# Partly accumulating transfers for the in-place additions of the last two layers, the last product cut in two, and a new order

## The chip, the cores and the metric

The kernel runs on one core of a Trainium2 chip. The metric is the time of one execution in device microseconds (us), the median of several runs. The core has a matrix engine (TensorE; PE in the profile, its weight loads PEld), VectorE (DVE), ScalarE (ACT) and GpSimd (POOL). SyncE (SP) issues the transfers between memory and the core. In the kernel before, GpSimd issues none.

## The reference

Three layers run one after the other on 2 batches of 768 tokens.

```
1. attention, 8 heads of 64: a window of +-15 keys, plus the maxima of 24 blocks of 32 keys; softmax; times v and block means
2. four causal attention experts of width 64 (q, k, v, output matrix); the two experts with the largest gate logits are summed
3. x_prev = x shifted by one token;  xk = mu_k*x + (1-mu_k)*x_prev,  xr likewise with mu_r
   k = max(xk @ w_k, 0);   v = (k*k) @ w_v;   out = sigmoid(xr @ w_r) * v
```

The third layer has 512 model columns and 1024 hidden ones. `w_k`, `w_v` and `w_r` come as 64-bit floats.

## The kernel before

All products keep nearly full precision: each operand is split into a rounded part and a rest (`halves`: a rounding, then a subtraction), and a product is three matmuls. The two large products of the third layer, `hid` (x times `w_k`) and `duo` (k*k times `w_v`), are built from seven products of half size in place of eight, with extra additions of operands and of partial results. A partial result comes out of one of eight PSUM banks by `copy` (ScalarE), `plus` or `plus_in` (VectorE, which alone adds from PSUM in these steps). Additions of two partial results that both lie in SBUF are `more(x, y)`, x += y: 8 for each of the two calls of `hid` (128 x 384 each) and 2 for each of the six calls of `duo` (128 x 256 each). `result` multiplies a finished quarter with the gate and stores it.

Every step is an operation with one or several ways to do it, an engine for each. `op` notes them in program order with what they read and write. `Plan.run` then issues them in the order of the list ORDER. An entry of ORDER divided by four is the number of the operation, and the remainder is its way. HOMES gives each buffer a place. Each engine runs its own instructions strictly in that order, and waits where an operand or a place isn't ready. The costs that the operations carry served the search for ORDER; they have no effect on the chip.

`more` was built with `both`, which has two ways, an addition on VectorE or the same on GpSimd. The last call of `duo` ends with a product of 256 columns (12 matmuls), `plus`, `result` and its store.

Of the kernel before, what the change touches and what calls it, by code (L numbers as in the profile page):

```python
# [20 lines left out]
P = 128  # L21
# [15 lines left out]
C = 384  # L37
# [277 lines left out]
def attn_moe_rwkv(  # L315
# [739 lines left out]
    def both(eng, dst, a, b, n, fn, r, w):  # L1055

        any_of(eng, [("dve", dve(n), lambda: nc.vector.tensor_tensor(dst(), a(), b(), fn), True),  # L1057
                     ("pool", pool_tt(n), lambda: nc.gpsimd.tensor_tensor(dst(), a(), b(), fn))], r=r, w=w)

    def flat64(w, k):  # L1060
        return raw64(w[k * P:(k + 1) * P].rearrange("p (m c) -> p m c", m=1))

# [423 lines left out]
```

## Time and profile before

| | |
|---|---|
| time, median of 3 runs | 333.79 us (331.25 to 334.03) |
| the profiled execution's own time | 333.63 us |
| its span, first to last instruction | 331.8 us |
| granted TensorE clock | 1.0 of full in the whole span |
| busy: TensorE, VectorE, ScalarE, GpSimd | 95%, 93%, 81%, 32% |

The span is the time from the first to the last instruction; the execution's own time has 1.8 us around it. Busy shares count overlapping instructions of an engine once. A busy TensorE may still hold short waits, since matmuls are pipelined, so its chain and its waits are read beside it.

### The profile page before, as it was taken

The numbers are of one execution on the slowest core, as the hardware profiler recorded it, in microseconds if no ns is written. First come the engines' busy times: TensorE is split into PE (matmuls) and PEld (weight loads), VectorE is DVE, ScalarE is ACT, GpSimd is POOL, SyncE is SP. The second block draws the span as 40 slices with busy tenths as digits, with TensorE's granted clock in tenths as the row PEclk, the third lists the DMA queues.
The fourth block names the chain that finished last, engine by engine and source line by source line (L and its number), as shares of the span: only waits on it lengthen the run. The fifth ranks groups of instructions, "written<-read, shape, count | busy, mean of one in ns | idle before, by whom it ended". The sixth has DMA issues, their size and how long they took to land.

```text
span 331.8 us, 8988 instructions
## 1 busy us (share of the span) xinstructions
PE 314.3 (95%) x3296; PEld 284.9 (86%) x3296; DVE 309.4 (93%) x936; ACT 267.6 (81%) x779; POOL 107.6 (32%) x128
## 2 busy tenths in 40 slices
PE   0769999999999999999999999999999999999995
PEld 0659998888799879888777899999997899999994
DVE  1988999999999899999999999999999999999995
ACT  1687989999999979597988897696997788967540
POOL 0563783784342632332400012142431302030121
PEclk9999999999999999999999999999999999999999
DMA  7996898854331101011212201000122000011123
GB/s 257 360 405 208 271 359 288 284 138 137 119 122 31 37 1 38 29 64 65 67 62 65 64 0 61 4 0 3 63 63 66 0 0 5 30 65 35 63 81 111
DMA packets 19735, 34.19 MB, mean 103 GB/s; under 512 B 2116, under 2 KB 8516, under 8 KB 19692
## 3 DMA queue, kind: packets, MB, share of 16 engines
q1 hardware_dynamic: 19692, 33.62, 30.6%
q8 instruction: 26, 0.43, 0.5%
q14 instruction: 17, 0.14, 0.1%
HBM read 30.13 MB, written 3.15 MB: 100 GB/s over the span
## 4 chain that ended last, share of the span: by engine, by line
PE 78%; DVE 16%; issue 2%; DMA 2%; ACT 1%; SPq 0%; DVEq 0%
PE ps L1282 18%; PE ps L752 11%; PE ps L1144 10%; PE ps L635 6%; PE ps L950 6%; PE ps L770 6%; PE ps L852 6%; PE ps L992 5%; PE ps L677 4%; PE ps L1195 4%; PE ps L581 3%; DVE b L376 2%; DVE t L1121 2%; DVE b L1057 2%; DMA ks<-in_kS 2%
## 5 line engine op out<-in xcount | busy, mean ns | idle before, releaser
L1282 PE MATMUL ps<-w,s 128*128 128x256 f32 x336 | 48.6, 281 | 0.0
L1282 PEld LDWEIGHTS ps<-w,s 128*128 128x128 f32 x336 | 43.9, 188 | 0.1
L1195 PE MATMUL ps<-b,w 128*128 128x384 f32 x216 | 40.6, 337 | 0.0
L368 ACT ACTIVATE t<-ps 128x192 f32<-128x192 f32 (+1 forms) x109 | 31.1, 347 | 9.6 <-PE ps L635 5.3
L1195 PEld LDWEIGHTS ps<-b,w 128*128 128x128 f32 x216 | 38.1, 188 | 0.1
L752 PE MATMUL ps<-b,w 128*128 128x384 f32 x192 | 37.3, 341 | 0.0
L1144 PE MATMUL ps<-w,b 128*128 128x512 f32 x144 | 35.5, 397 | 0.6 <-DVE b L1168 0.6
L752 PEld LDWEIGHTS ps<-b,w 128*128 128x128 f32 x192 | 33.1, 188 | 0.6 <-issue 0.2
L1144 PEld LDWEIGHTS ps<-w,b 128*128 128x128 f32 x144 | 26.5, 188 | 6.9 <-DVE b L1168 1.0
L368 ACT ACTIVATE b<-ps 128x384 f32<-128x384 f32 (+4 forms) x55 | 26.0, 489 | 6.7 <-PE ps L1195 2.7
L607 ACT ACTIVATE w<-w,nm 128x120 f32<-128x120 f32 x72 | 27.9, 391 | 0.0
L378 POOL TENSOR_TENSOR b<-t,b 128x384 fp32r<-128x384 f32 x7 | 9.2, 1315 | 49.5 <-DVE b L369 33.3
L368 ACT ACTIVATE b<-t 128x384 fp32r<-128x384 f32 x40 | 20.1, 522 | 4.9 <-DVE t L1121 2.5
L852 PE MATMUL ps<-ks,b 64*128 64x384 f32 (+3 forms) x192 | 21.0, 341 | 0.0
L368 ACT ACTIVATE s<-u 128x512 fp32r<-128x512 f32 x24 | 14.7, 625 | 7.8 <-DVE u L1057 5.3
L1121 DVE SCALAR_TENSOR_TENSOR t<-b,mu,t 128x384 f32<-128x384 f32 x32 | 20.9, 669 | 0.0
L368 ACT ACTIVATE w<-ps 120x256 f32<-120x256 f32 (+2 forms) x50 | 19.5, 430 | 1.6 <-PE ps L635 0.9
L950 PE MATMUL ps<-t,b 128*64 128x384 f32 (+2 forms) x144 | 20.8, 422 | 0.0
L376 DVE TENSOR_TENSOR b<-t,b 128x384 fp32r<-128x384 f32 x37 | 20.4, 563 | 0.0
L770 PE MATMUL ps<-q,b 128*128 128x260 f32 x144 | 19.7, 287 | 0.0
L992 PE MATMUL ps<-u,w 128*128 128x384 f32 x96 | 19.6, 339 | 0.0
L770 PEld LDWEIGHTS ps<-q,b 128*128 128x128 f32 x144 | 18.3, 188 | 0.6 <-issue 0.3
(200 smaller groups left out, 896.8 us busy)
## 6 DMA issues: line engine op xcount, KB each, us to landing
s<-in_wk SPq DMA_DIRECT2D x8, 512.0 KB, 4.0
s<-in_wv SPq DMA_DIRECT2D x8, 512.0 KB, 3.8
w<-in_vp SPq DMA_DIRECT2D x15, 256.0 KB, 6.1
w<-in_qT SPq DMA_DIRECT2D x12, 256.0 KB, 5.3
out_y<-t SPq DMA_DIRECT2D x24, 128.0 KB, 1.7
s<-in_wr SPq DMA_DIRECT2D x4, 512.0 KB, 5.5
s<-in_kS SPq DMA_DIRECT2D x6, 320.0 KB, 6.0
ks<-in_kS SPq DMA_DIRECT2D x4, 400.0 KB, 6.1
```

Of the source, the lines that this page charges most:

```text
L368: ways = [("act", act(n, sb), lambda: nc.scalar.activation(dst(), src(), AF.Copy)), ("dve", dve2(n) if sb else dve(n), lambda: nc.vector.t ...
L376: ways = [("dve", dve(n), lambda: nc.vector.tensor_tensor(dst(), a(), b().bitcast(F32), ALU.subtract), sb)]
L607: op("act", act(NK, True) + 186, lambda i=i, z=z, pr=pr, nm=nm: nc.scalar.activation(pr()[:, i], pr()[:, i], AF.Exp, bias=nm.t[:, i:i + 1] ...
L752: mm(p.t[:, :C], a[kc].t[:, cols], x.t[:, kc, :], start=(kc == 0 and i == 0), stop=(kc == KC - 1 and i == 2))
L770: mm(p.t[:, :260], x.t[:, kc, tok], a[kc].t, start=(kc == 0 and i == 0), stop=(kc == KC - 1 and i == 2))
L852: mm(ps[e2].t[:, :z - a], q1.t[r, x, tok], ks.t[r, y, a:z], start=n == 0, stop=n == 2)
L950: mm(acc.t[64 * e2:64 * e2 + 64, tq0 * P:(tq0 + cnt) * P], vv.t[:, kb, e * D:(e + 1) * D], th[e2].t[:, i0 * P:(i0 + cnt) * P], start=first ...
L992: mm(p.t[:, :C], a[ep].t[:, m * P:(m + 1) * P], x.t[:, ep, :], start=(ep == 0 and i == 0), stop=(ep == 1 and i == 2))
L1121: op("dve", dve(C) + 60, lambda: nc.vector.scalar_tensor_tensor(tmp(), cur(), mu.t[:, i:i + 1], tmp(), ALU.mult, ALU.add), r=rd, w=[(mb, m ...
L1144: mm(p.t, a.t[:, kc, tok], w[2](), start=(kc == 0 and i == 0), stop=(kc == KC - 1 and i == 2))
L1195: mm(p.t[:, :C], a[2]()[:, o:o + P], x.t[:, u, j], start=not (j or i), stop=j == 1 and i == 2)
L1282: mm(p.t[:, :256], x.t[:, u, j * P:(j + 1) * P], v[2]()[:, col:col + 256], start=not (j or i), stop=j == FC // 2 - 1 and i == 2)
```

## The change

1. `more` is built with a new `onto`, which has a third way: a transfer issued by GpSimd that adds y onto x on its way into x. It is noted with 900 ns on GpSimd and 4500 ns more until x can be used.
2. The last product of the last `duo` is cut into two of 128 columns, each with its own `plus`, `result` and store.
3. The cost of the score matmuls of layer 2 for the search is lowered and their kind is named "scores" in place of "rows".
4. ORDER and HOMES are new.

```
+    def onto(x, y, n):
+
+        any_of("dve", [
+            ("dve", dve(n), lambda: nc.vector.tensor_tensor(x[2](), x[2](), y[2](), ALU.add), True),
+            ("pool", pool_tt(n), lambda: nc.gpsimd.tensor_tensor(x[2](), x[2](), y[2](), ALU.add)),
+            ("pool", 900, lambda: nc.gpsimd.dma_start(x[2](), y[2](), accum_op=ALU.add), False, 4500.0),
+        ], r=[y[:2]], w=[x[:2]])
...
-                    op("pe", max(3 * pe_r(z - a) + 107.0, 385.0), go,
+                    op("pe", max(3 * pe_r(z - a), 330.0), go,
...
         def more(x, y):
-            both("dve", x[2], x[2], y[2], C, ALU.add, [y[:2]], [x[:2]])
+            onto(x, y, C)
...
         def more(x, y):
-            both("dve", x[2], x[2], y[2], 256, ALU.add, [y[:2]], [x[:2]])
+            onto(x, y, 256)
...
-        plus(u2, product(operand(s), 1, 256), 256)
-        result(ta, 256, u2)
+        n = P if tb == B * TPB - 1 else 256
+        x = operand(s)
+        for col in range(0, 256, n):
+            y = (u2[0], col, lambda col=col: u2[2]()[:, col:col + n]) if n < 256 else u2
+            plus(y, product(x, 1, 256 + col, n), n)
+            result(ta, 256 + col, y, n)
```

Of the 28 additions, 20 have remainder 2 in the new ORDER, so they become transfers: 14 of the 16 in `hid` (entries 5866, 5906, 5870, 5886, 5846, 5910, 5890, 5850 in the first call, 6414, 6434, 6378, 6398, 6418, 6438 in the second) and 6 of the 12 in `duo` (7322, 7326, 7658, 7662, 7826, 7830). Before, 16 of these 20 were on VectorE and 4 on GpSimd. These lines of the new list hold three of them (5890, 5850, 6414) and 5968, the `plus` that reads what 5890 has added to:

```
+    6032, 6132, 6904, 5780, 5890, 6236, 6921, 6016, 6104, 7056, 5850, 6177, 6140, 5784, 6220, 7060, 5952, 6152,
+    6340, 6144, 6020, 6160, 6004, 7064, 6024, 6241, 7068, 5964, 6036, 6448, 7148, 6445, 5976, 6228, 5968, 6630,
...
+    6710, 7009, 7124, 6742, 7025, 6364, 5948, 6408, 7028, 6384, 6744, 6414, 6200, 7156, 6192, 6368, 6480, 7100,
```

In the whole kernel, the two lists name these numbers of instructions: TensorE 2740 before and 2752 after (matmuls and transposes), VectorE 776 and 765 operations, ScalarE 581 and 571, GpSimd 124 and 144 (20 of them the transfers), SyncE 118 and 122 transfers.

## Rows read from the trace of the kernel before

**Rows 1.** The page: busy time of each engine, and two engines in 40 slices.
```profile
PE 314.3 (95%) x3296; PEld 284.9 (86%) x3296; DVE 309.4 (93%) x936; ACT 267.6 (81%) x779; POOL 107.6 (32%) x128
...
PE   0769999999999999999999999999999999999995
...
DVE  1988999999999899999999999999999999999995
```

**Rows 2.** The chain that ended last: start us, us, what, in order of time.
```profile
1.64 5.60 DMA ks<-in_kS
7.27 2.55 DVE ksm L487 x3
...
15.56 1.63 issue
...
21.95 2.23 issue
...
107.63 1.05 PE ps L992 x6
...
124.76 1.25 PE ps L992 x6
...
214.65 1.40 DVE ks L1168 x3
...
253.91 12.06 PE ps L1144 x51
...
270.89 56.99 PE ps L1282 x480
```

**Rows 3.** Windows of two stretches of `hid`: busy us of each engine, clock, DMA.
```profile
220.00:230.00 10.00, 10.00 (x59) 10.00 (x58) 10.00 (x19) 8.67 (x19) 3.97 (x4) 1.00 0.01 2
230.00:240.00 10.00, 9.65 (x55) 9.32 (x54) 10.00 (x21) 8.53 (x19) 3.78 (x3) 1.00 0.16 52
```

**Rows 4.** Waits of TensorE's matmuls from 24 us on, all of them: total, times, longest.
```profile
PE ps L581 <- issue: 2.2, 1, 2.2
PE ps L1144 <- DVE b L1168: 0.6, 1, 0.6
PE ps L1195 <- DVE b L1213: 0.4, 1, 0.4
```

**Rows 5.** Additions, by line and shape, 200 to 271 us: busy us, mean ns.
```profile
L1057 DVE TENSOR_TENSOR b<-b,b 128x384 f32<-128x384 f32 x9 | 5.6, 641 | 0.0
...
L1058 POOL TENSOR_TENSOR b<-b,b 128x384 f32<-128x384 f32 x3 | 4.4, 1467 | 14.7 <-DVE b L1057 8.9 <-DVE ks L1213 5.8
...
L1168 DVE TENSOR_TENSOR b<-ps,b 128x384 f32<-128x384 f32 x15 | 7.5, 542 | 0.0
```

**Rows 6.** GpSimd's additions of 128 x 256 by line, 230 to 271 us.
```profile
L1058 POOL TENSOR_TENSOR s<-s,s 128x256 f32<-128x256 f32 x2 | 5.1, 2526 | 9.7 <-DVE s L1057 9.7
```

**Rows 7.** The same in `duo`, 271 to 332 us, and VectorE's there.
```profile
L1058 POOL TENSOR_TENSOR t<-t,w 128x256 f32<-128x256 f32 x4 | 3.5, 881 | 12.0 <-DVE t L1057 12.0
...
L1057 DVE TENSOR_TENSOR t<-t,t 128x256 f32<-128x256 f32 x12 | 5.0, 419 | 0.1
```

**Rows 8.** The page's DMA issues: KB each, median us from issue to landing.
```profile
s<-in_wv SPq DMA_DIRECT2D x8, 512.0 KB, 3.8
w<-in_vp SPq DMA_DIRECT2D x15, 256.0 KB, 6.1
...
out_y<-t SPq DMA_DIRECT2D x24, 128.0 KB, 1.7
```

**Rows 9.** The timeline of the end: start us, us, engine, line, operation.
```profile
327.59 0.28 PE L1282 MATMUL ps<-u,s 128*128 128x256 f32 x1
327.90 0.42 DVE L1168 TENSOR_TENSOR t<-ps,t 128x256 f32<-128x256 f32 x1
328.36 0.42 DVE L1057 TENSOR_TENSOR t<-t,w 128x256 f32<-128x256 f32 x1
```

**Rows 10.** TensorE by line and shape, whole span: the smallest score matmuls.
```profile
L852 PE MATMUL ps<-ks,b 64*128 64x128 f32 x24 | 2.2, 280 | 0.0
```

**Rows 11.** VectorE's timeline ahead of a wait of TensorE.
```profile
251.00 0.41 DVE L1035 TENSOR_SCALAR s<-s 128x512 f32<-128x512 f32 x1
...
251.80 1.25 DVE L1039 TENSOR_SCALAR s<-s 128x512 int32<-128x512 int32 x1
```

More of the change, by code (lines that the diff above doesn't have):

```diff
@@ L238, in op @@
         o = Op()
-        o.ways = [(*w, w[0] == "pool")[:4] for w in [(eng, cost, fn, lock or eng == "pool")] + list(ways)]
+        o.ways = [w if len(w) > 4 else (*w, w[0] == "pool")[:4] for w in [(eng, cost, fn, lock or eng == "pool")] + list(ways)]
         o.eng, o.seq, o.late, o.issue = eng, len(self.ops), late, issue
@@ L852, in go @@
                                 mm(ps[e2].t[:, :z - a], q1.t[r, x, tok], ks.t[r, y, a:z], start=n == 0, stop=n == 2)
-                    op("pe", max(3 * pe_r(z - a) + 107.0, 385.0), go,
+                    op("pe", max(3 * pe_r(z - a), 330.0), go,
                        r=[(q1, (ep, 0)), (q1, (ep, 1))] + [(ks, (ep, q, hf)) for hf in range(half + 1) for q in range(2)],
-                       w=ps, stream="p2", claim=prs + nms, mode="rows")
+                       w=ps, stream="p2", claim=prs + nms, mode="scores")
                     for e2 in range(2):
@@ L1273, in duo, with product @@
         a11, a12, a21, a22 = piece(ta, 0), piece(ta, 1), piece(tb, 0), piece(tb, 1)
-        def product(x, w, col):
+        def product(x, w, col, n=256):
             p = bank("ps")
@@ L1281, in go @@
                     for i, (u, v) in enumerate(((0, h), (0, l), (1, h))):
-                        mm(p.t[:, :256], x.t[:, u, j * P:(j + 1) * P], v[2]()[:, col:col + 256],
+                        mm(p.t[:, :n], x.t[:, u, j * P:(j + 1) * P], v[2]()[:, col:col + n],
                            start=not (j or i), stop=j == FC // 2 - 1 and i == 2)
-            op("pe", 12 * pe_r(256), go, r=[x] + [v[:2] for j in range(FC // 2) for v in wvp[j][2 * w:2 * w + 2]],
+            op("pe", 12 * pe_r(n), go, r=[x] + [v[:2] for j in range(FC // 2) for v in wvp[j][2 * w:2 * w + 2]],
                w=[p], stream="p3")
@@ L1294, in plus_to @@
         def plus_to(p, y):
-            x = part("t", 256, F32)
+            x = (part("t", 256, F32)[0], None, lambda: x[0].t)
             op("dve", dve(256), lambda: nc.vector.tensor_tensor(x[2](), p.t[:, :256], y[2](), ALU.add), r=[p, y[:2]],
@@ L1300, in more, with result @@
         def more(x, y):
-            both("dve", x[2], x[2], y[2], 256, ALU.add, [y[:2]], [x[:2]])
-        def result(t, col, x):
+            onto(x, y, 256)
+        def result(t, col, x, n=256):
             rb, rk, ra = rg[t]
             row = t * P
-            both("dve", x[2], x[2], lambda: ra()[:, col:col + 256], 256, ALU.mult, [(rb, rk)], [x[:2]])
-            op("sp", dma(P * 1024), lambda: nc.sync.dma_start(out[row:row + P, col:col + 256], x[2]()), r=[x[:2]])
+            both("dve", x[2], x[2], lambda: ra()[:, col:col + n], n, ALU.mult, [(rb, rk)], [x[:2]])
+            op("sp", dma(P * 4 * n), lambda: nc.sync.dma_start(out[row:row + P, col:col + n], x[2]()), r=[x[:2]])
         (cb, ck, ca), (db, dk, da) = part("u3", dt=F32), part("u3", dt=F32)
```

276 rows, old and new, of tables (HOMES, ORDER) are left out of this document.

## The prediction, made before the change was run

> **What bounds the kernel now.** I read the page first, then the chain, then windows of the stage that the change is about, and last the waits of TensorE. On the page [rows 1] TensorE's row is at 9 from the third slice on; VectorE's is too, so both could be the bound. The chain tells them apart by stretch [rows 2]: a head of loads, maxima and two gaps (1.63 and 2.23 us) for which the trace names no releaser; then TensorE; pieces of VectorE such as the 1.40 us one at 214.65 only between about 201 and 254 us, which is `hid`; and from 253.91 on TensorE without a break, the last 56.99 us being the 480 matmuls of `duo`. But in `hid` TensorE is full as well [rows 3]: 59 matmuls of 384 columns in 10 us are 0.170 us each, and elsewhere six such take 1.05 us [rows 2], 0.175 each. So where the chain names VectorE, TensorE hardly loses by it. How much it loses is in its waits [rows 4]: from 24 us on its matmuls waited for data 0.6 + 0.4 = 1.0 us (the 2.2 us is the second gap of the head). The granted clock is 1.00, the 2.4 GHz level [rows 3]. So TensorE's own work is the bound, and the change leaves that work as it is, but for the last product. What can be won is about 1 us of waits, changes of kind, the head and the tail.
>
> **The additions.** Twenty become transfers. Sixteen of them were on VectorE, 10 in `hid` and 6 in `duo`: 10 x 0.64 [rows 5] + 6 x 0.42 [rows 7] = 8.9 us of VectorE's 309.4 [rows 1]. The new list gives other operations back to it: 776 become 765, so 11 fewer, not 16. All of that lies beside a full TensorE, so it is worth only the waits that VectorE ends: 1.0 us in all [rows 4], and both waits are for it. I take 0.6 off, with bounds of 1.0 off and, as a new order brings its own waits, 1.0 on. Four additions leave GpSimd, 4 x 1.47 = 5.9 us [rows 5], and 20 issues come. GpSimd is busy 3.97 and 3.78 us in 10 [rows 3]. Even at 2.5 us, its dearest addition [rows 6], 14 issues are 35 us, which fits into the 50 us of `hid`, though barely.
>
> What a transfer takes from issue to use no row shows. From below, a store of 128 KB lands in 1.7 us [rows 8] (an addition in `hid` moves 192 KB); from above, a load takes 6.1 us [rows 8], and GpSimd may be late by as much as one of its additions is in `hid` against `duo`, 2.53 - 0.88 = 1.6 us [rows 6, 7]: 7.7 us. I take 3.8, the load of 512 KB [rows 8], because it runs in the same stage and twice 192 KB are read. What covers it is VectorE's queue. Between entry 5890 and 5968, the `plus` that needs its result, the new list has 11 VectorE operations (6921, 6104, 6177, 6220, 7060, 6340, 6020, 7064, 6241, 7068, 6448): 11 x 0.54 [rows 5] = 6.0 us. 6414 and 6434 have 11 too; the other additions of VectorE's queue have more. In GpSimd's own queue the second addition of a pair waits for the first to land (6438 for 6434 after 10 VectorE operations, 7326 for 7322 after 9), and behind it stand subtractions of `halves` that feed TensorE. At 3.8 us all is hidden, so I count nothing. If the cover were gone, VectorE would stand at that `plus`, behind it every emptying of a bank, and behind these TensorE.
>
> One rule speaks against the change. The same addition of 128 x 256 takes GpSimd 2.53 us in `hid` and 0.88 in `duo` [rows 6, 7], and a VectorE shift takes 1.25 us [rows 11] where its neighbour of like size takes 0.41: the two engines hold each other up. The Trainium skill, "SBUF — State Buffer", section "A bandwidth-pool intuition that's wrong (but worth ruling out)", says that a transfer issued by GpSimd that took about 620 ns alone took about 3100 ns beside a VectorE copy, because GpSimd can't write its descriptors while VectorE holds the shared port. The rows agree that the engines block each other; none shows it of a transfer. By that rule, some 2.5 us more, an estimate, the 3.8 would be 6.3 us, just over the cover, and the first rival would begin. The skill's "DMA: Bandwidth & Descriptors", section "Anatomy of one DMA — SWDGE (gpsimd) path", prices a transfer alone at about 2.0 us plus its bytes at 436 GB/s, 2.45 us for 192 KB by estimate; by that the cover would hold even so (4.95 us). No run here shows either.
>
> **The order.** The list is new from its first entries, for all layers. TensorE's work stays; what it loses at changes of kind does not. Counting in both lists how often it goes from one kind (full products, transposes, scores of layer 2, value products, scores and block means of layer 1) to another, I find 102 before and 96 after. Six matmuls of one line took 1.25 us right behind scores and 1.05 amid full products [rows 2], 0.2 us for one change at the most. I take 0.1 x 6 = 0.6 us off, bounds 0 and 1.2. In the head the key tile that VectorE wants first is now loaded first. It stood waiting until 7.27 [rows 2]; the four loads took 5.60 us together, 1.4 each. I take 0.3 off, bounds 0 and 1.0, because the last maximum still waits for the last load. The two gaps stay: the same kinds of matmuls come there. SyncE's four more transfers are three small copies and the second store; its queue is short there, so nothing. The lowered cost of the score matmuls changes no instruction.
>
> **The tail.** The product of 12 matmuls of 256 columns at 56.99 / 480 = 0.119 us [rows 2] takes 1.42 us. As 24 of 128 columns it costs the same if time goes with columns, and 1.42 us more if each still takes 0.119. Between them: the smallest score matmuls are at 2.2 / 24 = 0.092 us busy [rows 10]; that share counts run-outs (`duo`'s counted so are at 0.145 for 0.119), so some 0.075, x 24 = 1.8 us. I take +0.4. After the last matmul there follow `plus` and the gate's product, 0.42 us each [rows 9]; 128 columns fewer save 0.12 each (0.54 for 384 against 0.42 for 256 [rows 5, 7]), so -0.25. The first half's two steps and store hide beside the second half's matmuls, else they cost 0.6. Net +0.15, bounds -0.25 and +1.2.
>
> **The sum.** -0.6 - 0.6 - 0.3 + 0.15 = -1.35 us on the profiled execution's own 333.63 (span 331.8 and 1.8 around it; the median is 333.79, nearly the same): 332.3 us. With the bounds 330.2 to 335.8.
>
> **Rivals.**
> - *The transfers come late* (slower). Place: the `plus` behind 5890, 6414 and 6434 and the second of each pair in GpSimd's queue; point: an issue-to-use time above 6.0 us. At the upper bound of 7.7 each of five groups (two calls of `hid`, three of `duo`) would stand 1.7 us: 8.5 us, about half if the eight banks let TensorE run on. 332.3 + 4.3 to 8.5; I take 338. For it: the engines' mutual stretching [rows 6, 7, 11]. Against it: the 3.8 and 1.7 us rows [rows 8].
> - *The new order waits elsewhere.* A list for all layers that fits the real durations less well: stretched steps like the 1.25 us one [rows 11] come at other places. One such step cost TensorE 0.6 us [rows 4]; four to seven more give 334.7 to 336.5. For it: VectorE is at 10.00 of 10 us [rows 3], without slack.
> - *Everything goes right* (faster by over 1%). No data waits (-1.0), the full price for changes of kind (-1.2), the head's bound (-1.0), the tail's (-0.25), and a quarter of the two gaps (-1.0): 329.2. Against it: it needs all at once, since TensorE's work is the floor.
> - *Nothing can be seen*: VectorE's time is freed where TensorE is full. That is within my forecast.
>
> **How the numbers follow.** Runs of the kernel before spread from 331.25 to 334.03, so 1% (3.3 us) is about what a measurement can tell. Forecast 332.3, with 330.6 to 334.4: 0.58. Late transfers 0.15, waits elsewhere 0.12, everything right 0.15. The range from 329.6 to 337.0 leaves out half of the late case and a part of the best one. Faster by over 1% (below 330.45) is the best case, 0.15; slower by over 1% (above 337.1) most of the late one and a little of the other, 0.14; the rest 0.71.
>
> **What would show it.** If I am right, TensorE's chain is unbroken through `duo`, its waits for data after 24 us stay under 2 us, VectorE's busy time falls by 5 to 9 us without the span following, and the additions land within 6 us. Wrong: waits of VectorE at `plus` or of GpSimd released by a transfer; the two gaps of the head gone or longer; matmuls of 128 columns at 0.119 us each.

## The result, and the profile after

The changed kernel takes 336.69 us (median of 8 runs, 334.76 to 337.15), the kernel before 333.62 in the same comparison (8 runs, 331.25 to 334.96): a ratio of 1.0091 [1.0063, 1.0119], 3.0 us slower by the ratio. I had said 332.3 us and 329.6 to 337.0: the time lies in the range, but on the other side of the kernel before. The profiled execution took 336.56 us, its span is 334.8 us. Three parts of its page: busy times, the granted clock in 40 slices, the chain by engine.

```profile
PE 319.5 (95%) x3308; PEld 289.6 (87%) x3308; DVE 309.0 (92%) x925; ACT 265.4 (79%) x772; POOL 121.7 (36%) x148
...
PEclk9998999999999999999999999999999999999999
...
PE 90%; DVE 4%; DMA 2%; issue 2%; ACT 1%; SPq 0%; DVEq 0%; ACTq 0%
```

Against [rows 1] VectorE has 11 instructions fewer and is busy just as long, where I had expected 5 to 9 us less: its steps became longer. GpSimd, with 20 instructions more, is busy 14 us more. The waits of TensorE's matmuls from 24 us on, which answer to [rows 4]:

```profile
PE ps L853 <- DVE nm L860: 1.2, 1, 1.2
PE ps L753 <- DVE b L377: 0.6, 1, 0.6
PE ps L853 <- ACT t L369: 0.2, 1, 0.2
```

Both waits of [rows 4] for VectorE, in `hid`, are gone, and new ones stand elsewhere: for row maxima of layer 2's scores (L860) at 47 us and for a subtraction of `halves` (L377) at 33 us. The windows that answer to [rows 3] have TensorE full and VectorE with a little slack:

```profile
220.00:230.00 10.00, 10.00 (x59) 10.00 (x59) 9.90 (x20) 8.71 (x20) 4.81 (x6) 1.00 0.41 92
230.00:240.00 10.00, 10.00 (x59) 10.00 (x58) 9.57 (x21) 9.84 (x23) 2.92 (x3) 1.00 0.01 2
```

The transfers among the DMA issues (KB each, median us to landing), which [rows 8] had to stand in for, and `hid`'s issues on GpSimd by shape (busy us, mean ns):

```profile
b<-b POOLq DMA_DIRECT2D x10, 192.0 KB, 3.7
...
b<-ks POOLq DMA_DIRECT2D x4, 192.0 KB, 3.6
t<-t POOLq DMA_DIRECT2D x6, 128.0 KB, 3.0
```

```profile
L1066 POOL DMA_DIRECT2D b<-b x10 | 9.4, 1063 | 8.7 <-ACT b L369 5.6 <-DVE ks L1222 3.0
L1066 POOL DMA_DIRECT2D b<-ks x4 | 4.5, 1206 | 0.0
```

I had taken 3.8 us. VectorE waits for none of them from 180 us on; GpSimd waits for one twice, 4.7 us in all, with nobody behind it.

To see where the time went I set the traces side by side at equal progress of TensorE: each of its steps counts with the usual length of its kind (the lower quartile over all traces), and where the sums are equal the clock times are compared. The table is worked out so from the traces of all runs; it gives us later (+) or earlier (-) than the kernel before, by the time in the trace before (the labels are those of the next section). Up to about 26 us executions differ by a microsecond or two either way, whatever the list. At 52 and 78 us the lists do different work, and there the numbers depend by up to 1 us on how the steps are counted.

```
time in the trace before     26     35     52     78    110    120    215    236    257    317
the change                -0.80   1.31   2.92   2.82   2.94   3.74   3.90   3.24   2.40   2.20
early_after               -1.51   0.39   1.98   2.91   3.19   3.18   3.26   3.42   3.43   3.27
late_after                -0.44   0.29   0.26   0.33   0.32   0.32   0.52  -0.16  -1.04  -1.28
late_add_back             -0.12  -0.09  -0.12  -0.12  -0.11  -0.11   0.13   2.08   1.75   2.01
before_transfers          -1.87  -0.35  -0.38  -0.37  -0.38  -0.38  -0.38   5.03   4.86   5.83
gating_later              -1.24   0.12   0.69   1.30   1.42   2.20   2.33   1.69   0.84   0.73
```

Four more traces have the new list in the early part too (steps_later with the edit of gating_later). Counted matmul by matmul they give:

```
time in the trace before     35    110    120    215    317
add_back                  -0.88  -0.09   0.72   0.87   3.14
add_none                   2.54   3.49   4.29   4.47   2.77
after_uncut                1.08   3.99   4.80   4.97   3.28
steps_later                1.47   3.89   4.68   4.82   3.23
```

The change loses some 3 us before 52 us, in layer 1 and the first projections, where no addition and no transfer of the change lies; 0.8 us at 110 to 120 us; wins 1.5 us between 215 and 257 us, in `hid`; and the cut product at the end, which is behind the table's last column, takes most of that again. The 0.8 us are lost in all seven traces that have the new list there and in none of the six that have the old one. The early loss is not the same in every execution: add_back, with the same entries up to there, has none of it at 110 us, and after_uncut has 4.0 us.

### The profile page after: what moved, and what is told of

It reads as the page before. It is cut to its first block, busy times and chain, and to the rows that moved or that the text cites. A ratio compares the mean times of both kernels' runs of the same rounds, so it can differ in the third digit from the quotient of the medians.

```text
span 334.8 us, 9045 instructions
## 1 busy us (share of the span) xinstructions
PE 319.5 (95%) x3308; PEld 289.6 (87%) x3308; DVE 309.0 (92%) x925; ACT 265.4 (79%) x772; POOL 121.7 (36%) x148
## 4 chain that ended last, share of the span: by engine, by line
PE 90%; DVE 4%; DMA 2%; issue 2%; ACT 1%; SPq 0%; DVEq 0%; ACTq 0%
PE ps L1291 18%; PE ps L1204 18%; PE ps L1153 10%; PE ps L753 9%; PE ps L951 6%; PE ps L636 5%; PE ps L853 5%; PE ps L993 5%; PE ps L771 4%; PE ps L678 3%; PE ps L582 3%; DMA ks<-in_kS 2%; PE ps L587 1%; PE ps L502 1%; ACT w L369 1%
## 5 line engine op out<-in xcount | busy, mean ns | idle before, releaser
L1291 PE MATMUL ps<-w,s 128*128 128x256 f32 (+1 forms) x348 | 50.1, 280 | 0.0
L1291 PEld LDWEIGHTS ps<-w,s 128*128 128x128 f32 x348 | 45.4, 188 | 0.3
L1204 PE MATMUL ps<-b,w 128*128 128x384 f32 x216 | 41.8, 338 | 0.0
L753 PE MATMUL ps<-b,w 128*128 128x384 f32 x192 | 37.3, 340 | 0.6 <-DVE b L377 0.6
L369 ACT ACTIVATE t<-ps 128x192 f32<-128x192 f32 (+1 forms) x112 | 31.3, 347 | 5.6 <-PE ps L636 3.4
L753 PEld LDWEIGHTS ps<-b,w 128*128 128x128 f32 x192 | 33.2, 188 | 1.3 <-DVE b L377 0.9
L369 ACT ACTIVATE b<-ps 128x384 f32<-128x384 f32 (+4 forms) x50 | 24.3, 496 | 9.3 <-PE ps L993 2.7
L379 POOL TENSOR_TENSOR b<-t,b 128x384 fp32r<-128x384 f32 x10 | 12.7, 1266 | 41.6 <-ACT b L369 41.3
L377 DVE TENSOR_TENSOR b<-t,b 128x384 fp32r<-128x384 f32 x34 | 20.5, 610 | 1.0 <-ACT b L369 0.9
L369 ACT ACTIVATE b<-t 128x384 fp32r<-128x384 f32 x36 | 18.2, 519 | 3.9 <-DVE t L1130 2.3
L369 ACT ACTIVATE s<-u 128x512 fp32r<-128x512 f32 x24 | 14.8, 627 | 7.9 <-PE ps L1291 5.8
L369 ACT ACTIVATE w<-ps 120x256 f32<-120x256 f32 (+2 forms) x45 | 17.9, 434 | 2.8 <-DVE w L370 1.7
L379 POOL TENSOR_TENSOR w<-s,w 128x512 fp32r<-128x512 f32 x11 | 14.5, 1317 | 12.9 <-DVE w L370 4.5
```

What stands on the lines that cost most here:

```text
L369: ways = [("act", act(n, sb), lambda: nc.scalar.activation(dst(), src(), AF.Copy)), ("dve", dve2(n) if sb else dve(n), lambda: nc.vector.t ...
L377: ways = [("dve", dve(n), lambda: nc.vector.tensor_tensor(dst(), a(), b().bitcast(F32), ALU.subtract), sb)]
L379: ways.append(("pool", pool_tt(n), lambda: nc.gpsimd.tensor_tensor(dst(), a(), b().bitcast(F32), ALU.subtract)))
L753: mm(p.t[:, :C], a[kc].t[:, cols], x.t[:, kc, :], start=(kc == 0 and i == 0), stop=(kc == KC - 1 and i == 2))
L1204: mm(p.t[:, :C], a[2]()[:, o:o + P], x.t[:, u, j], start=not (j or i), stop=j == 1 and i == 2)
L1291: mm(p.t[:, :n], x.t[:, u, j * P:(j + 1) * P], v[2]()[:, col:col + n], start=not (j or i), stop=j == FC // 2 - 1 and i == 2)
```

## The experiments

All ratios are to the kernel before, with 95% intervals. First I took the three parts asunder, then the list by stretches, then single steps of it.

**add_back.** All 20 additions back on VectorE, at their places in the new list (twenty entries, as 5866, less two):

```
-    5836, 6964, 5866, 6064, 5740, 6056, 6125, 5916, 5348, 5336, 5681, 5716, 5756, 5341, 5496, 6128, 5744, 6116,
+    5836, 6964, 5864, 6064, 5740, 6056, 6125, 5916, 5348, 5336, 5681, 5716, 5756, 5341, 5496, 6128, 5744, 6116,
```

> The changed kernel with its 20 transfers put back on VectorE at the same places of the list. Theory A (TensorE's work is the bound, the transfers are hidden and free VectorE, the loss comes from the new early order and the cut product): VectorE gets 14 x 0.55 + 6 x 0.42 = 10.2 us back in stages where it has 0.3 to 0.9 us free in 20, so TensorE waits again: 1.5 to 5 us slower than the changed kernel, 338 to 342 us. Theory B (the transfers cost the time): 1 to 3 us faster than the changed kernel, 333.5 to 335.5 us.

338.15 us, 1.0142 [1.0099, 1.0186]: slower still by 0.5%, so the transfers are not the loss.

**add_none.** The 20 additions left out, neither issued nor done elsewhere:

```
-            ("pool", 900, lambda: nc.gpsimd.dma_start(x[2](), y[2](), accum_op=ALU.add), False, 4500.0),
+            ("pool", 900, lambda: None, False, 4500.0),
```

> The changed kernel with the 20 additions left out, neither transferred nor computed. Theory A: nothing waits for the transfers, so leaving them out is worth at most 0.5 us: 336 to 337 us. Theory B: the loss goes with them, 333 to 335 us.

336.79 us, 1.0081 [1.0038, 1.0123]: with the transfers or without them, the time is the same. They cost nothing in this list.

**before_transfers.** The list of the kernel before, the same 20 additions as transfers at their old places (5905 becomes 5906, 5844 becomes 5846, and so on).

> The kernel before with its own list, but the same 20 additions as transfers at the places where the list has them. Theory A: the two waits of TensorE for VectorE in the third layer (1.0 us by the waits, 1.7 us by the matmuls' starts) go, if the list leaves the transfers about 4 us before they are needed: 0.5 to 1.7 us faster than the kernel before, 332 to 333 us. Theory B: 1 to 3 us slower than it, 334.5 to 336.5 us.

339.81 us, 1.0174 [1.0134, 1.0213], 5.8 us slower: a miss. Its trace shows why; VectorE's waits from 180 us on:

```profile
DVE ks L1176 <- DMA b<-ks: 7.9, 3, 3.7
DVE t L1057 <- DMA t<-t: 4.5, 1, 4.5
DVE b L1176 <- DMA b<-b: 1.5, 1, 1.5
```

and its chain, start and length in us, runs over five transfers:

```profile
209.13 3.02 DMA b<-b
213.75 4.43 DMA b<-b
...
223.13 3.02 DMA b<-ks
...
250.18 3.32 DMA b<-b
...
316.45 2.66 DMA t<-t
```

The transfers are no longer than in the changed kernel (medians of 3.6, 3.0 and 2.7 us to landing), but here the next reader stands right behind them. The rival of late transfers is real; the new list is what keeps it away.

**after_uncut.** The change with the last product whole:

```
-        n = P if tb == B * TPB - 1 else 256
+        n = 256
```

> The changed kernel with the last product whole, one step to empty it, one gate product and one store. Theory A: 24 matmuls of 128 columns took 2.7 us against 1.42 us for 12 of 256, and the end behind them was 0.4 us shorter, so 0.5 to 0.9 us faster than the changed kernel, about 336.0 us. Theory C (the cut product is the loss): about 3 us faster.

336.19 us, 1.0053 [1.0017, 1.0089]: 0.5 us by the medians, 1.3 us by the ratios, for the cut; the interval overlaps the change's, so the times alone don't show it.

**before_cut.** The other way round, the list of before with its last product cut at the same place (two entries more).

> The kernel before with its last product alone cut into two halves of columns, at the same place of the list. Theory A1: slower by 0.5 to 0.9 us, 334.1 to 334.5 us, since the 24 half-width matmuls take longer than the 12 whole ones by more than the shorter last steps save. Theory C (the cut is most of the loss of 3 us): 336 us.

333.76 us, 1.002 [0.9994, 1.0047]: 0.7 us, not clear of noise. Its trace ends with matmuls and steps of 256 columns, so in that list the cut product isn't the last to run, and only its price shows, not its gain.

So most of the loss is left for the order. Three kernels join the two lists (the places of some 100 buffers in HOMES follow), all with the last product whole.

**early_before.** The list of before for its first 416 entries (about 56 us), then the new one, transfers included.

> The last product is whole here; the list of the kernel before stands for its first 416 entries (about 56 us), the changed list for all the rest, transfers included. Theory A1 (some 3 us are lost in the first 56 us of the changed list, where TensorE's clock falls to a half for 3.4 us and VectorE's steps are stretched beside GpSimd's, and 1.5 us are won back behind 200 us): about 333 us, a ratio to the kernel before of 0.997 to 1.003. Theory D (the loss comes from the later parts of the changed list or from the transfers): 336 us, as the changed list with the whole last product had it.

333.99 us, 1.0012 [0.9987, 1.0037]. With the early part of before, 0.4% of after_uncut's 0.53% is gone, although the seam costs a wait of its own (TensorE 1.6 us for L369).

**early_after.** The first 412 entries of the new list, then the list of before.

> The last product is whole; the changed list stands for its first 412 entries (about 56 us), the list of the kernel before for all the rest, and no addition is a transfer. Theory A1: the early loss alone, with nothing won back: 336 to 337 us, a ratio of 1.008 to 1.010. Theory D: as the kernel before, 333 to 334 us.

335.83 us, 1.0056 [1.0027, 1.0084]: 1.9 us lost with nothing else of the change in it, less than forecast and than the 3 us of the profiled traces. So the early part of the list costs time by itself. Between 24 and 70 us TensorE waits under the new list for more than one thing: in early_after's trace for a load and for row maxima, in after_uncut's for a step of ScalarE and for a subtraction:

```profile
PE ps L677 <- DMA u<-in_vp: 1.5, 1, 1.5
PE ps L852 <- DVE nm L859: 1.1, 1, 1.1
```

```profile
PE ps L581 <- ACT omu L423: 1.3, 1, 1.3
PE ps L752 <- DVE b L376: 0.5, 1, 0.5
```

The trace of steps_later has both of the long ones (1.1 and 1.4 us), that of the kernel before neither.

**late_after.** The list of before for its first 1440 entries (about 192 us), then the new one.

> The last product is whole; the list of the kernel before stands for its first 1440 entries (about 192 us), the changed list with its 20 transfers behind that. Theory A1: the gain of the last two layers alone: about 332 us, a ratio of 0.993 to 0.997, the fastest of all. A rival, that the additions by transfer are of no use under any list: 333 to 334 us.

331.8 us, 0.9954 [0.9926, 0.9981]: faster than both kernels, by 1.5 us against before.

**late_add_back.** As late_after, all 20 additions on VectorE.

> The list of the kernel before for its first 1440 entries and the changed list behind that, the last product whole, and all 20 additions done by VectorE in place at the places of the list where the transfers stood. If the transfers are what makes the changed order of the last two layers pay: 333.4 to 335.7 us, 1.6 to 3.9 us over the same list with transfers (331.8 us), so no faster or slower than the kernel before. If the order alone pays: 331.8 us as with them.

335.48 us, 1.0049 [1.0024, 1.0075]. Under the new order of `hid` and `duo` the transfers are worth 0.9954 against 1.0049, 3.2 us; the two were timed in different sessions, each against the kernel before. The windows of both kernels from 200 to 260 us, of late_after and then of late_add_back (columns as in [rows 3]):

```profile
200.00:260.00 60.00, 60.00 (x331) 58.20 (x331) 57.45 (x118) 50.32 (x109) 28.52 (x29) 1.00 0.37 73
```

```profile
200.00:260.00 60.00, 58.44 (x317) 55.25 (x316) 59.45 (x124) 46.21 (x100) 16.47 (x14) 1.00 0.08 27
```

With the additions VectorE is full and TensorE does 317 matmuls; without them, 331.

What else loses the time early? In the changed kernel's trace the timeline of VectorE, GpSimd and TensorE around the wait for L860 reads:

```profile
45.95 1.27 DVE L814 TENSOR_TENSOR cc<-gl 128x48 f32<-128x48 f32 x1
47.14 0.15 DVE L812 TENSOR_REDUCE mx<-gl 128x3 f32<-128x12 f32 x1
47.21 0.41 DVE L370 COPY w<-ps 120x256 f32<-120x256 f32 x1
47.54 0.28 DVE L860 CUSTOM_DVE_ANT_0 w<-ps,w 128x128 f32<-128x128 f32 x1
...
45.71 1.44 POOL L379 TENSOR_TENSOR w<-s,w 128x512 fp32r<-128x512 f32 x1
...
46.34 0.38 PE L853 MATMUL ps<-ks,b 64*128 64x256 f32 x1
47.88 1.15 PE L853 MATMUL ps<-ks,b 64*128 64x256 f32 x11 [1.16 <-DVE nm L860]
```

A step of 48 columns for the gates takes 1.27 us beside GpSimd's subtraction, and behind it in VectorE's queue stand the row maxima that empty the banks of the scores. The twelve score matmuls take 2.7 us from 46.34 to 49.03. In the list of before these gate steps come behind the maxima.

**gating_later.** The changed kernel with the three gate steps (1104, 1108, 1100) behind the five maxima (the last is 1864):

```
-    740, 1380, 1188, 1092, 888, 1104, 892, 3612, 1372, 196, 896, 1108, 1816, 942, 1100, 909, 905, 1484, 901, 1824,
-    1480, 912, 1526, 1820, 1836, 1376, 944, 1489, 1856, 1493, 1844, 1832, 1840, 1532, 1500, 1496, 1864, 1848, 3616,
+    740, 1380, 1188, 1092, 888, 892, 3612, 1372, 196, 896, 1816, 942, 909, 905, 1484, 901, 1824, 1480, 912, 1526,
+    1820, 1836, 1376, 944, 1489, 1856, 1493, 1844, 1832, 1840, 1532, 1500, 1496, 1864, 1104, 1108, 1100, 1848, 3616,
```

> The changed kernel whole, with one edit of its list: three small steps of VectorE for the gates (two products of 128x48 and a maximum, at 45.1 to 47.2 us of the changed trace) stand behind the five row maxima of the scores instead of ahead of them, as they do in the list of the kernel before. Theory E (the early loss is VectorE reaching the row maxima late, because such steps stand ahead of them and are stretched beside GpSimd): TensorE's wait of 1.2 us at L853 at about 47 us goes, the two scores steps there take 0.5 us each in place of 1.9 and 0.7, and the time falls by 0.4 to 1.6 us, to 335.1 to 336.3 us. Theory F (the early loss is TensorE's clock and the loads, whatever VectorE's order): no change, 336.7 us.

334.82 us, 1.0049 [1.0013, 1.0084], 0.42% or 1.4 us better than the change, as forecast, but the two intervals overlap; steps_later below, with the same edit in it, is 1.0 us better. The maxima, the gate steps and the matmuls there now:

```profile
44.79 0.28 DVE L860 CUSTOM_DVE_ANT_0 w<-ps,w 128x128 f32<-128x128 f32 x1
...
46.99 0.20 DVE L813 TENSOR_TENSOR cc<-gl 128x48 f32<-128x48 f32 x1
47.11 0.20 DVE L814 TENSOR_TENSOR cc<-gl 128x48 f32<-128x48 f32 x1
...
44.61 1.29 POOL L379 TENSOR_TENSOR w<-s,w 128x512 fp32r<-128x512 f32 x1
...
45.15 1.15 PE L853 MATMUL ps<-ks,b 64*128 64x256 f32 x12
```

GpSimd's subtraction is still there, but beside it VectorE now works on steps that read PSUM, and these keep their length. The twelve matmuls take 1.15 us here and 1.19 in steps_later. With the gate steps ahead they took 2.7 us in the change and in early_after, where L814 ran 1.27 us, but only 1.6 to 1.7 in add_back, after_uncut and add_none, where it ran 0.62 us or less. Add_back's:

```profile
43.33 0.62 DVE L814 TENSOR_TENSOR cc<-gl 128x48 f32<-128x48 f32 x1
...
44.14 1.62 PE L853 MATMUL ps<-ks,b 64*128 64x256 f32 x12
```

So these steps cost TensorE 0.5 to 1.5 us, by how GpSimd's steps fall beside them.

**steps_later.** As gating_later, and a subtraction of 128 x 512 (4501), 1.79 us at 112.86 us in the changed trace, behind the copies that TensorE needs (behind 3492).

> As the run before, and one more step of VectorE is moved back, the subtraction of 128x512 that takes 1.79 us at 112.86 us beside a GpSimd subtraction in the changed trace (0.68 us elsewhere): it stands behind the copies that TensorE's transposes and scores at 115 to 117 us wait for. Theory E: TensorE wins another 0.4 to 0.8 us between 109 and 121 us, so 334.5 to 335.8 us in all, a ratio of 1.002 to 1.006. Theory F: 336.7 us.

335.99 us, 1.0062 [1.0031, 1.0093], and between 110 and 120 us TensorE loses 0.8 us as before (3.89 to 4.68 in the table): a miss. Up to 110 us its list is that of gating_later, whose trace is 2.5 us ahead there; so much differs from execution to execution. Its timeline of VectorE and GpSimd tells why the move won nothing:

```profile
113.81 1.51 DVE L1036 TENSOR_SCALAR s<-s 128x512 f32<-128x512 f32 x1
...
116.51 0.68 DVE L377 TENSOR_TENSOR s<-s,s 128x512 fp32r<-128x512 f32 x1
...
113.58 1.46 POOL L379 TENSOR_TENSOR w<-s,w 128x512 fp32r<-128x512 f32 x1 [4.54 <-DVE w L370]
```

The subtraction is at 0.68 us, but the next step, 0.41 us in the trace of the change, now stands beside the same GpSimd step and takes 1.51. The blockage has only changed its victim; both read only SBUF.

**gating_earlier.** The kernel before with its gate steps ahead of the maxima (1104, 1108, 1100 behind 1376).

> The kernel before, with its three gating steps of VectorE moved ahead of the row maxima of the scores, where the changed list has them. Theory E: the kernel before gets a wait of TensorE for the row maxima at about 45 us, 0.3 to 1.4 us, and ends at 334 to 335 us. Theory F, or cover that the list of before has there: no change, 333.3 to 333.6 us.

335.5 us, 1.0028 [0.9993, 1.0062]: inconclusive by the time. The trace shows 0.7 us lost there by TensorE (from 0.83 to 1.53 us at 48 us), within the forecast, and a step of the gate of 0.53 us beside GpSimd. The median's 2 us are more than that; 9 of its 12 runs have a mean granted clock below 0.997, but 13 of the 35 of the kernel before beside them.

## Why the prediction was wrong

**What bounds it: right.** TensorE's work is the bound. Leaving out the 20 additions changed nothing (add_none), and where the change waits, TensorE loses at once. That the time lies in my range is luck: the range's upper part was put there for late transfers, which did not come.

**The additions: right that they are hidden, too small a gain.** Landing was put at 3.8 us and measured 3.6 to 3.7 for 192 KB and 3.0 for 128; the cover of 11 VectorE operations held, and nobody that matters waited. I took 0.6 us off; late_after, transfers and new order of `hid` and `duo` together, shows 1.5, and of these two the transfers alone are worth 3.2 (late_add_back). The term looked only at the waits that the list of before had, with VectorE's time worth nothing beside a full TensorE; in an order that leaves VectorE full it is worth time. The rival of late transfers needs 6 us in the new list, but in the list of before it came at once (before_transfers). The Trainium skill's rule on descriptors ("SBUF — State Buffer", section "A bandwidth-pool intuition that's wrong (but worth ruling out)"), by which the prediction estimated 6.3 us, didn't show itself: the issues took 1.06 to 1.21 us each in `hid` and 0.87 in `duo`, and the medians to landing stayed below 3.8.

**The order: the step that failed.** I priced the new list by its changes of kind (-0.6) and by the head's first load (-0.3), and left the waits that it could bring to a bound of 1.0 us under the additions and to a rival with a chance of 0.12, at 334.7 to 336.5. That rival is nearest to what happened, though it took all such waits for stretched steps of VectorE at 0.6 us each, and the traces hold waits of 0.6 to 1.5 us, for loads and ScalarE too. In the chain the head's load takes 6.38 us against 5.60 [rows 2], one gap of 1.97 us is left of the two, and the first matmul starts at 6.04 us in place of 4.84; what that cost was caught up by 26 us, so the head gave nothing, and no gain from fewer changes of kind shows in the table. Instead early_after lost 1.9 us with the first 412 entries, of which the gate steps are 0.5 to 1.5 by the traces. The traces add 0.8 us at 110 to 120 us. The sum by the runs is 1.9 + 0.8 - 1.5 + 0.7 to 1.3 for the cut, 1.9 to 2.5 us; the measured 3.0 us lie 0.5 to 1.1 above, within what intervals of half a per cent leave open. In the two profiled executions the sum closes: 2.2 us at 317 us in the table and 0.9 for the tail, against 3.0 between their spans. The sign that I should have read is in my own rows: a shift stretched to 1.25 us ahead of a wait of TensorE [rows 4, 11]. Such steps don't vanish with a new order, and that one stands ahead of a bank that TensorE wants can be read from the two lists before any run: the gate steps ahead of the maxima are such a place. Whether a step of GpSimd then runs beside it the lists don't say: L814 took 1.27 us in one execution and 0.62 in another.

The same step of VectorE shows the stretching plainly. Before, with GpSimd idle until 31.08 us:

```profile
29.78 0.69 DVE L376 TENSOR_TENSOR w<-s,w 128x512 fp32r<-128x512 f32 x1
30.39 0.42 DVE L376 TENSOR_TENSOR q<-b,q 128x260 fp32r<-128x260 f32 x1
```

After, ahead of the wait at L753:

```profile
30.40 1.31 DVE L377 TENSOR_TENSOR q<-b,q 128x260 fp32r<-128x260 f32 x1 [0.32 <-ACT q L369]
31.63 1.09 DVE L377 TENSOR_TENSOR w<-s,w 128x512 fp32r<-128x512 f32 x1
...
32.84 0.68 DVE L377 TENSOR_TENSOR b<-ps,b 128x512 fp32r<-128x512 f32 x1
...
30.14 1.28 POOL L379 TENSOR_TENSOR w<-s,w 128x512 fp32r<-128x512 f32 x1 [2.07 <-ACT w L369]
31.39 1.81 POOL L372 TENSOR_SCALAR w<-s 128x512 fp32r<-128x512 f32 x2
```

The step that began 0.26 us behind GpSimd's ends 0.29 us behind it (31.71 against 31.42); the one that reads PSUM keeps 0.68 us. The Trainium skill, "SBUF — State Buffer", section "Who interferes with whom", says that a VectorE instruction with two SBUF inputs contends with a GpSimd instruction that reads SBUF, and that the shared port pair is an exclusive lock. The trace agrees, with these numbers.

**The clock is not the cause.** In the changed trace the granted clock fell to a half, the 1.2 GHz level, from 24.48 to 27.89 us, behind a gap of TensorE of 1.97 us; the window of 24 to 28 us:

```profile
24.00:28.00 4.00, 4.00 (x80) 3.88 (x80) 2.98 (x12) 3.08 (x8) 2.00 (x3) 0.57 1.02 378
```

I first took that for a part of the loss. But late_after, the fastest kernel, has the same fall,

```profile
24.00:28.00 4.00, 4.00 (x82) 3.88 (x80) 2.39 (x9) 1.28 (x4) 0.47 (x1) 0.57 0.93 322
```

and early_after lost its 2 us at full clock:

```profile
24.00:28.00 4.00, 3.72 (x88) 3.52 (x84) 3.90 (x12) 4.00 (x14) 2.07 (x3) 1.00 0.98 344
```

What the clock does do is blur single numbers. Of the kernel before, the 47 runs with a mean granted clock of 0.997 or more took 333.0 us in the mean, the 31 others 334.8. Against these means, sorted alike, the change is 3.2 and 1.8 us slower (4 runs each), early_after 2.7 and 1.7 (8 and 2 runs), and late_after 2.6 and 2.5 faster (2 and 9 runs).

**The tail: mis-sized.** The net of +0.15 us measured 0.7 (before_cut) to 1.3 (after_uncut's ratio), neither clear of noise by itself. The rows size it. The term of the matmuls was +0.4; in before_cut's trace more matmuls follow the 24 halves, so that they can be timed from start to start:

```profile
323.81 2.79 PE L1290 MATMUL ps<-w,s 128*128 128x128 f32 x24
326.44 0.33 PE L1290 MATMUL ps<-p,s 128*128 128x256 f32 x1
```

They take 326.44 - 323.81 = 2.63 us, 0.110 each against 0.119 for 256 columns [rows 2]: +1.2, near my upper bound. The last steps did become shorter by 0.13 each, as I had it, so the net is +0.9:

```profile
331.29 0.29 DVE L1177 TENSOR_TENSOR t<-ps,t 128x128 f32<-128x128 f32 x1 [0.72 <-PE ps L1291]
331.62 0.29 DVE L1058 TENSOR_TENSOR t<-t,w 128x128 f32<-128x128 f32 x1
```

**What stays open.** What is left of the early loss behind gating_later is some 0.5 us by the ratios and 1.4 us at 110 us by its trace; why executions of one list lose 0 to 4 us there, with waits for loads and ScalarE in some and not in others, no run settles. The 0.8 us at 110 to 120 us are placed, but not undone: the one step that I moved there only handed its wait on.

## What to carry to other kernels

A new order is a term of its own: where the list is new, look in it for VectorE steps that read only SBUF, may run beside GpSimd and stand ahead of something that empties a bank for TensorE, and price each at up to the length of the GpSimd step; three small steps ahead of the maxima cost TensorE 0.5 to 1.5 of the 3 us. One trace of a list is one execution: traces of the same early list lay 4 us apart, so set the medians of runs beside it. A transfer that adds takes time off VectorE for nothing only where the list leaves it 4 us before its result is read; the same twenty were worth 3.2 us in one list and cost 5.8 in the other. Cut a last product only if its narrower matmuls cost less than the shorter last steps give back (here 1.2 us against 0.26), and time the stretches of a new list apart: only the part from 192 us on was worth having here.

## What the runs showed of the hardware that I had not expected

- A matmul of 128 columns is hardly shorter than one of 256: 0.110 us from start to start (before_cut) against 0.119.
- An accumulating transfer from SBUF to SBUF issued by GpSimd takes 3.6 to 3.7 us for 192 KB and 3.0 for 128 KB to land, and its issue 0.87 us of GpSimd, 1.06 to 1.21 where GpSimd and VectorE are busier.
- A VectorE step of 128 x 48 took 1.27 us beside a GpSimd subtraction and 0.20 without; one of 128 x 512 with a single SBUF input took 1.51 against 0.41.
- The granted clock fell to a half for 3.4 us behind gaps of TensorE of 1.7 to 2.5 us in seven of the fourteen traces, and not in others with such a gap: the trace of before has one of 2.23 us [rows 2] and the full clock, and early_after has the change's 1.97 us and the full clock. Runs with a lower mean clock took 1.8 us longer in the kernel before.
